# Agent attention and a SoLU feed-forward layer in one kernel: copies of u for float32r transposes, an earlier split of p, a new head, a new place for a product, and a new order

## The chip, the cores and the metric

The kernel runs on one core of one Trainium2 chip. The metric is device time in microseconds (us) of one execution. Before the change the median of three runs is 1497.92 us, the lowest 1496.82 and the highest 1499.42.

## The reference, cut to what matters

There are 4 batches of 12608 tokens with 128 channels, and 49 agents. The 50432 rows that come out of the attention go through a layer of width 1024.

```python
scale = 1 / sqrt(128)
def sm(a, b):                       # softmax of scaled products
    s = scale * (a @ b.T); e = exp(s - s.max(-1)); return e / (e.sum(-1) + 1e-9)
agent_v = sm(agents, k) @ v         # 49 x 128 for each batch
x = sm(q, agents) @ agent_v         # 12608 x 128 for each batch
h = x @ w_in                        # 50432 x 1024
solu = h * softmax(h)
ln = (solu - mean) / sqrt(var + 1e-6) * g_ln
out = ln @ w_out                    # 50432 x 128
```

## The kernel before, in words

**Algebra.** The kernel never forms x. For each batch it forms M = agent_v @ w_in (49 x 1024) and then h = p @ M, where p is the softmax of q against the agents. M is kept as a high and a low part, `mh` and `ml`, in float32r (the form of float32 that TensorE takes in one pass), and p as a high and a low part stacked on the partitions. The mean and the gain of the normalisation are folded into w_out (`w2`, and its parts `wH` and `wL`), so that only the factor of each row (from the sums S and Q of `c_exp` and `c_sq`) is left for the end.

**Phase a** (`phase_a`), once for each batch: 13 chunks of k and v. Products with k into PSUM (L465), maximum on VectorE, exponential on ScalarE (L491), transposes (L498), a copy (L504), products with v (L514). For batch 0 (the head) the loads of k and v go in turn, one chunk of each, into borrowed buffers.

**Phase b** (`phase_b`), once for 8 tiles of 128 tokens: products of q with the agents (L694), softmax on VectorE and ScalarE, the product with the reciprocal on GpSimd into `pack` (L722), two float32 transposes for 4 tiles (L729), a copy on ScalarE (`pf`, L737), the split into high and low on GpSimd (L743, L748), and 4 transfers that put the parts into place in `pT` (L767).

**The main loop** goes over 396 tiles of 128 tokens. For a tile x: `c_h` (L824, four float32r products with 512 columns into one of two PSUM tiles `ph`), `c_max` on VectorE (L828), `c_exp` on ScalarE (L838), `c_u` on VectorE (L843: u = h times e), `c_sq` on ScalarE (L849). Then u must be transposed and multiplied by w_out, and there are two ways. Pairs of tiles alternate between them, four tiles make a unit:

- Z tiles (204): `c_t` transposes u with eight 128x128 float32 transposes on TensorE (L856) into two of four PSUM banks `px`; `c_ev` copies them to SBUF on ScalarE (L907); GpSimd splits them into `uH` (L916) and `uL` (L920); `c_w` multiplies a pair of tiles by `wH` and `wL` in 24 float32r products of 256 columns (L937). The output comes out transposed, so the factor of a token stands along the row: `c_rstd` computes it on GpSimd, transposes it on VectorE (L976), sends it to DRAM (L980) and broadcasts it back to all partitions as `rB` (L984). `c_fin` on VectorE multiplies the PSUM bank by `rB` (L1020), which frees the bank, and `c_out` stores it (L1025).
- Y tiles (192): VectorE transposes u in 32x32 blocks (`c_tb`, L863), 16 transfers move the blocks into place (`c_mv`, L871), `c_wy` multiplies in plain float32 (L877, two passes for each of 32 products in a unit). The factor stands on the partitions here; it gets there by a product on GpSimd (`y0`, L1002), a small product on TensorE (`y1`, L1007) and a copy (`y2`, L1011), and `c_fy` applies it on ScalarE or VectorE (L885, L887).

The last 16 tiles have halves that are split directly from PSUM (`c_ldir`), and the last unit takes its factor through TensorE (`d0`, `d1`, `d2`).

**What sets the order.** All of this is registered as operations of a planner (`Plan`). Each has an engine, a cost, a due time, dependencies, and whether it takes or frees one of the four PSUM banks. The planner simulates the engines, including the queue of SyncE (SP), which issues all transfers, and emits each engine's instructions in the order it finds, and the engines keep that order. The due times are the constants `DH`, `DMX`, `DEX` and so on, each with values for the start and the end; `SWITCH`, `HOLD` and `EPS` say how TensorE changes between kinds of work. The planner's cost for four transposes of u is 0.435.

Of the kernel before, what the change touches and what calls it, by code (L numbers as in the profile page):

```python
# [19 lines left out]
class Op:  # L20


    __slots__ = ("eng", "fn", "cost", "due", "left", "outs", "deps", "take", "free", "bank", "start", "end", "by", "ready", "kind", "shy")


class Plan:
# [8 lines left out]
    SWITCH = ((0.0, 0.0, 0.09), (0.0, 0.0, 0.09), (0.15, 0.12, 0.0))  # L35

    HOLD = 0.12

    def __init__(self, banks):
# [4 lines left out]
        self.kind = 0  # L44

# [14 lines left out]
    def push(self, o):  # L60
        o.ready = {}
        for e in o.eng:
            o.ready[e] = max([0.0] + [d.end + (self.LAT.get(d.by + e, 0.2) if d.by != "S" else 0.0) for d in o.deps])
            self.cand[e].append(o)

    def run(self, idle=None):
        while True:
            best = None
            for e, ops in self.cand.items():
                if not ops:  # L70
                    continue
                free = [b[0] for b in self.banks if b[0] is not None]
                first = min(free) if free else None
                at, opts, low = self.at[e], [], None
                for o in ops:
                    s = max(at, o.ready[e])
                    if o.take:
                        if first is None:
                            continue
                        s = max(s, first)  # L80
                    opts.append((s, o))
                    low = s if low is None else min(low, s)
                if low is None:
                    continue
                near = [z for z in opts if z[0] <= low + self.EPS[e]]
                if e == "P" and self.kind == 2:
                    near = [z for z in opts if z[0] <= low + self.HOLD and z[1].kind == 2] or near
                s, o = min(near, key=lambda z: z[1].due)
                if o.shy > 0.0:
                    s, o = min((z for z in opts if z[0] <= s + o.shy), key=lambda z: z[1].due)  # L90
                if best is None or s < best[0]:
                    best = (s, e, o)
            if best is None:
                break
            s, e, o = best
            for z in o.eng:
                self.cand[z].remove(o)
            if o.take:
# [5 lines left out]
            o.start, o.by = s, e  # L104
            if e == "S":
                hold, size, lag = o.cost
                self.at[e] = s + hold
# [43 lines left out]
def kernel(  # L151
# [25 lines left out]
    CPR = 5.63  # L177
    UTB = 3
# [7 lines left out]
    WC = 4  # L186

    BD0 = 5.03
    BD1 = 15.85
    BD2 = 1.88  # L190
    BD3 = -20.87
    BD4 = -3.24
    BD5 = 3.07
    DH = -9.08
    DMX = 6.59
    DEX = 1.64
    DU_ = -21.8
    DSQ = 15.3
    DT = -0.97
    DEV = 13.79  # L200
    DLD = 12.64
    DSP = 16.84
    DW = 13.2
    DR = 15.79
    DF_ = 37.93
    OUTD = 20.02
    OUTC = -69.6
    VA = 3
    VA1 = 12
    QA = 22.03  # L210
    WA = -7.03
    VLAG = 0.74
    PTB = 4
    SHY = 0.31
    DHR = 5.82
    DHL = -9.02
    DMXR = 19.87
    DMXL = 0.06
    DEXR = -2.43
    DEXL = -3.57  # L220
    DUR = -30.17
    DUL = 17.14
    DSQR = -54.86
    DSQL = 4.96
    DTR = -20.36
    DTL = -14.12
    DEVR = -17.55
    DEVL = 7.51
    DLDR = -20.48
    DLDL = -18.62  # L230
    DSPR = -1.34
    DSPL = -11.65
    DWR = -2.28
    DWL = 3.97
    RBL = 2.38
    ASP = 0.86
    MZ = 5.66
    B7G = True
    B7 = 7.35
    DTB = 4.24  # L240
    DMV = -0.75
    DMS = 0.0
    MVC = 2
    DWY = 11.65
    DWS = 4.05
    YC = 2
    DFY = 5.09
    DTBR = -5.14
    DTBL = -8.26
    ASTART = -4.09  # L250
    AEND = 0.95
# [8 lines left out]
    mpool = ctx.enter_context(tc.tile_pool(name="mpool", bufs=2))  # L260
    bpool = ctx.enter_context(tc.tile_pool(name="bpool", bufs=2))
    epool = ctx.enter_context(tc.tile_pool(name="epool", bufs=3))
    gpool = ctx.enter_context(tc.tile_pool(name="gpool", bufs=ZB))
    ypool = ctx.enter_context(tc.tile_pool(name="ypool", bufs=2))
# [7 lines left out]
    make_identity(nc, ident)  # L272
    ones = const.tile([P, P], F32, name="ones")
# [13 lines left out]
    def pair_f64(dst, names):  # L287
# [5 lines left out]
        def tmp():  # L293
            for k, tg in (("s", "e"), ("a", "e"), ("e", "u"), ("m", "u")):
                t = epool.tile([P, 2, HW], I32, tag=tg, bufs=2, name=f"c{k}_{names}")
                for h in range(2):
                    z[k, h] = t[:, h, :]
# [37 lines left out]
    def load_out():  # L335
        nc.sync.dma_start(out=g_sb, in_=g_ln)
        for h in range(2):
            wd = words["out", h] = mpool.tile([P, HW, 2], I32, tag="mh" if h == 0 else "ml", name=f"wd_out{h}")
# [6 lines left out]
    def conv_out():  # L345
# [8 lines left out]
        def sums(q):  # L354

            n = NF >> (q + 1)
            if q == 0:
                pm["s"] = epool.tile([P, NF // 2, C], F32, tag="sq", bufs=1, name="ws")
# [32 lines left out]
    for i in range(2):  # L391
        pk = const.tile([P, GT, AP2], F32, name=f"pack{i}")
        nc.gpsimd.memset(pk, 0.0)
        packs.append(pk)
# [9 lines left out]
    fold32 = const.tile([P, SQB], F32, name="fold32")  # L404
    nc.vector.tensor_reduce(out=fold32, in_=ident.rearrange("p (a c) -> p c a", c=SQB), op=ALU.add, axis=AX.X)
    quad = const.tile([P, GT], F32, name="quad")
    nc.vector.tensor_reduce(out=quad, in_=ident.rearrange("p (a c) -> p a c", c=SQB), op=ALU.add, axis=AX.X)
    ph2 = [ps_h.tile([P, DF], F32, name=f"ph{i}") for i in range(2)]
    plan = Plan([ps_x.tile([P, HW], F32, name=f"px{i}") for i in range(4)])
    op = plan.op  # L410
# [9 lines left out]
    def phase_a(b, due, gate):  # L420
# [14 lines left out]
        def kload(c):  # L435
            w = CT * P if c < NCK else CKT
            if not head:
                kts[c] = kpool.tile([C, CT * P], F32, tag="kt", name=f"kt{b}_{c}")
            else:
                if c % 4 == 0:  # L440
                    kts["t"] = ypool.tile([C, 4, CT * P], F32, tag="tb", name=f"kh{b}_{c}")
# [3 lines left out]
        def vload(c):  # L445
            if head:
                if c % 4 == 0:
                    vts["t"] = ypool.tile([P, 4, CT, C], F32, tag="uY", name=f"vh{b}_{c}")
# [51 lines left out]
        def p2_et(c, k="D"):  # L500
            px = ps.pop(("t", c))
            w = HW if c < NCK else TX
            eT = res["eT", c] = bpool.tile([P, HW], F32, tag="eT", name=f"eT{b}_{c}")
# [100 lines left out]
        def kop(c):  # L604
            if c < NC and c not in K:
                old = M1.get(c - 1) if not head else M1.get(c - 5 - c % 4)
                K[c] = op("S", st(kload, c), (0.45, sz(c), 0), -199 + 0.2 * c if head else at(c * 2.55 - 3), gate + [old])

        def vop(c):
            old = M2.get(c - 1) if not head else M2.get(c - 5 - c % 4)  # L610
# [4 lines left out]
        FC = {}  # L615
        for c in range(NC):
# [9 lines left out]
            if c:  # L626
                FC[c] = op("A", st(p1_fc, c), 0.2, at(z + 0.6), [N1[c], AC.get(c - 4)])
            TT[c] = op("P", st(p2_t, c), 0.435 * fr(c), at(z + 1), [EE[c], M2.get(c - 2)], take=True)
            ET[c] = (op("A", st(p2_et, c, "A"), 0.478 * fr(c), at(z + 1.2), [TT[c]], free=TT[c]) if head and c < HEADA else
                     op(ETE, st(p2_et, c), (0.478 * fr(c), 0.6 * fr(c)), at(z + 1.2), [TT[c]], free=TT[c]))  # L630
            vop(c)
            M2[c] = op("P", st(p2_mm, c), 0.88 if c < NCK else 0.42, at(z + MZ) if not head else at(z + 1.5),
                       [ET[c], V[c], M2.get(c - 1), AC.get(c - 2)], take=True, kind=2)
            AC[c] = op("D", st(p2_ev, c), 0.26, at(z + 1.8), [M2[c], FC.get(c), AC.get(c - 1)], free=M2[c])
# [17 lines left out]
        for hf in range(2):  # L652
            o8 = op("P", st(f3, hf), 0.86, at(z + 0.5 + 0.4 * hf), [fb] + cin, take=True)
            o9 = op("A", st(f4h, hf), 0.571, at(z + 0.8 + 0.4 * hf), [o8, l0, last_h.get(b - 2)] + mdone[b])
# [26 lines left out]
    def phase_b(k, dues, gate=()):  # L681
# [36 lines left out]

        def b4(q):
            m = min(GT, nt - q * GT)  # L720
            sl = slice(q * GT, q * GT + m)
            nc.gpsimd.tensor_tensor(out=packs[q][:, :m, :A], in0=r["d"][:, sl, :],  # L722
                                    in1=r["s"][:, sl].unsqueeze(2).to_broadcast([P, m, A]), op=ALU.mult)

        def b5(q, px):
            m = min(GT, nt - q * GT)
            r["pt", q] = px
            for j in range(0, m, 2):
                nc.tensor.transpose(px[:, j * AP2 : (j + 2) * AP2], packs[q][:, j : j + 2, :].rearrange("p j a -> p (j a)"),  # L729
                                    ident)  # L730

        def b6(q):
            w = (min(GT, nt - q * GT) + 1) // 2 * P
            r["n", q] = bpool.tile([P, 2, GT // 2 * P], F32R, tag="pn", bufs=2, name=f"pn{b}_{t0}_{q}")
            if B7G:
                r["f", q] = bpool.tile([P, GT // 2 * P], F32, tag="pf", bufs=2, name=f"pf{b}_{t0}_{q}")
                nc.scalar.copy(out=r["f", q][:, :w], in_=r.pop(("pt", q))[:, :w])  # L737
            else:
                nc.scalar.copy(out=r["n", q][:, 0, :w], in_=r["pt", q][:, :w])

        def b7h(q):
            w = (min(GT, nt - q * GT) + 1) // 2 * P
            nc.gpsimd.tensor_scalar(out=r["n", q][:, 0, :w], in0=r["f", q][:, :w], scalar1=1.0, scalar2=0.0, op0=ALU.mult, op1=ALU.add)  # L743

        def b7l(q):
# [498 lines left out]
```

## Time and profile before

| | us |
|---|---|
| median of 3 runs (lowest, highest) | 1497.92 (1496.82, 1499.42) |
| the profiled execution's own time | 1496.0 |
| span of that execution in the trace | 1494.2 |
| TensorE (PE) busy | 1447.1 |
| VectorE (DVE) busy | 1371.5 |
| ScalarE (ACT) busy | 1291.3 |
| GpSimd (POOL) busy | 1110.3 |

The span goes from the first to the last instruction, and the execution's own time has 1.8 us around it. PE's busy time is modelled, since its instructions overlap: for PE one reads how far apart instructions start, and the idle time. PEld are the loads of the stationary operand. Of a wait, the profile gives what ended it. Line numbers (L856) are those of the kernel before.

### The profile page before, as it was taken

The page shows a single profiled execution, that of the slowest core. Times are in us where ns is not written, and L with a number is a line of the kernel's source. Part 1 is how long each engine was busy: PE and PEld are TensorE (multiplying, and loading weights), DVE is VectorE, ACT ScalarE, POOL GpSimd, SP SyncE. Part 2 cuts the span into 40 slices and gives each one's busy share as a digit, 9 for nine tenths or more (in the row PEclk, how much of TensorE's full clock was granted, in tenths as well). Part 3 has the DMA queues.
Part 4 walks back from the last instruction along what each step waited for, and adds up shares of the span by engine and source line. Part 5 has one row for each costly group of instructions (what it writes and reads, how often), then busy time and mean ns, then how long its engine had stood idle before and what let it go on. Part 6 is the DMA issues. An engine that isn't in the chain of part 4 may idle for free.

```text
span 1494.2 us, 34108 instructions
## 1 busy us (share of the span) xinstructions
PE 1447.1 (97%) x11954; PEld 1285.0 (86%) x11954; DVE 1371.5 (92%) x1987; ACT 1291.3 (86%) x2536; POOL 1110.3 (74%) x1569
## 2 busy tenths in 40 slices
PE   8889999999999999999999999899999999999999
PEld 5668889898988989989887888789889898989998
DVE  7799999999999999999998898699999999999996
ACT  4688989889988988899887898688899999999995
POOL 2667787788778777787786677677788888888875
PEclk9999999999999999999999999999999999999999
DMA  9565676676577668756657655567546656566461
GB/s 371 163 179 156 177 186 160 174 184 153 144 194 202 165 179 215 181 137 158 155 140 200 184 156 157 147 175 206 138 118 157 152 126 166 137 154 162 114 155 57
DMA packets 142698, 247.72 MB, mean 166 GB/s; under 512 B 26048, under 2 KB 80320, under 8 KB 142528
## 3 DMA queue, kind: packets, MB, share of 16 engines
q1 hardware_dynamic: 142528, 245.54, 63.1%
q8 instruction: 96, 1.57, 0.5%
q14 instruction: 74, 0.61, 0.1%
HBM read 92.77 MB, written 26.05 MB: 80 GB/s over the span
## 4 chain that ended last, share of the span: by engine, by line
PE 56%; ACT 13%; DVE 10%; DMA 10%; issue 5%; SPq 4%; POOL 2%; DVEq 0%; ACTq 0%; POOLq 0%
PE ph L824 15%; PE px L877 14%; PE px L937 11%; PE px L856 6%; ACT e L838 5%; DVE u L843 4%; DMA rB<-dr 4%; ACT sq L849 4%; DVE nm L828 3%; PE px L465 3%; SPq L871 3%; PE px L514 3%; DMA dr<-yr 2%; ACT uT L907 2%; PE px L694 2%
## 5 line engine op out<-in xcount | busy, mean ns | idle before, releaser
L849 ACT ACTIVATE sq<-u,su 128x1024 bf16<-128x1024 f32 x396 | 460.7, 1163 | 53.4 <-DVE u L843 49.2
L843 DVE SCALAR_TENSOR_TENSOR u<-ph,e 128x1024 f32<-128x1024 f32 x396 | 474.6, 1217 | 29.4 <-ACT e L838 13.6
L838 ACT ACTIVATE e<-ph,nm 128x1024 f32<-128x1024 f32 x396 | 442.8, 1124 | 60.6 <-DVE nm L828 58.9
L828 DVE TENSOR_REDUCE nm<-ph 128x1 f32<-128x1024 f32 x396 | 467.8, 1206 | 28.2 <-PE ph L824 26.8
L920 POOL TENSOR_TENSOR uL<-uT,uH 128x1024 fp32r<-128x1024 f32 (+1 forms) x198 | 470.7, 2377 | 14.5
L877 PE MATMUL px<-w,uY 128*128 128x128 f32 x3072 | 383.0, 276 | 1.7 <-ACT uT L907 1.0
L877 PEld LDWEIGHTS px<-w,uY 128*128 128x128 f32 x3072 | 365.9, 192 | 8.7 <-ACT uT L907 2.3
L824 PE MATMUL ph<-mh,pT 128*128 128x512 f32 x792 | 336.5, 425 | 8.6 <-DVE u L843 5.4
L824 PE MATMUL ph<-ml,pT 128*128 128x512 f32 x792 | 312.8, 395 | 0.0
L916 POOL TENSOR_SCALAR uH<-uT 128x1024 fp32r<-128x1024 f32 (+1 forms) x198 | 207.6, 1048 | 99.2 <-ACT uT L907 99.0
L937 PE MATMUL px<-uH,wH 128*128 128x256 f32 x816 | 238.7, 292 | 0.6 <-POOL x L957 0.3
L863 DVE STREAM_TRANSPOSE tb<-u 128x1024 f32<-128x1024 f32 x192 | 237.2, 1238 | 1.3
L937 PE MATMUL px<-uL,wH 128*128 128x256 f32 x816 | 235.7, 289 | 0.0
L907 ACT COPY uT<-px 128x512 f32<-128x512 f32 x394 | 220.8, 595 | 16.7 <-PE px L856 12.9
L937 PE MATMUL px<-uH,wL 128*128 128x256 f32 x816 | 235.0, 288 | 0.0
L856 PE MATMUL px<-ident,u 128*128 128x128 f32 x1632 | 223.0, 274 | 6.8 <-DVE ob L1020 4.0
L856 PEld LDWEIGHTS px<-ident,u 128*128 128x128 f32 x1632 | 191.2, 141 | 33.4 <-DVE ob L1020 5.1
L824 PEld LDWEIGHTS ph<-mh,pT 128*128 128x128 f32 x792 | 149.8, 189 | 43.7 <-DVE u L843 13.5
L824 PEld LDWEIGHTS ph<-ml,pT 128*128 128x128 f32 x792 | 150.1, 189 | 19.5 <-DVE ml L590 0.3
L937 PEld LDWEIGHTS px<-uH,wL 128*128 128x128 f32 x816 | 153.8, 189 | 5.0 <-issue 2.3
L937 PEld LDWEIGHTS px<-uH,wH 128*128 128x128 f32 x816 | 153.9, 189 | 4.8 <-issue 1.3
L937 PEld LDWEIGHTS px<-uL,wH 128*128 128x128 f32 x816 | 154.1, 189 | 4.2 <-issue 1.1
(132 smaller groups left out, 1595.9 us busy)
## 6 DMA issues: line engine op xcount, KB each, us to landing
uY<-tb SPq DMA_DIRECT2D x768, 128.0 KB, 2.9
pT<-pn SPq DMA_DIRECT2D x392, 64.0 KB, 2.2
qt<-in_qT_dram SPq DMA_DIRECT2D x48, 512.0 KB, 4.4
kt<-in_kT_dram SPq DMA_DIRECT2D x36, 512.0 KB, 4.4
vt<-in_v_dram SPq DMA_DIRECT2D x36, 512.0 KB, 4.8
rB<-dr SPq DMA_DIRECT2D x50, 256.0 KB, 3.7
out_dram<-ob SPq DMA_DIRECT2D x50, 256.0 KB, 2.6
out_dram<-oy SPq DMA_DIRECT2D x48, 256.0 KB, 2.8
```

What stands on the lines that cost most here:

```text
L824: nc.tensor.matmul(ph[:, sl], lhs, bmats[b]["mh" if m == 0 else "ml"][:, sl], start=(m == 0), stop=(m == 1))
L828: nc.vector.tensor_reduce(out=nms[x], in_=phs[x], op=ALU.max, axis=AX.X, negate=True)
L838: nc.scalar.activation(out=es[x], in_=phs[x], func=AF.Exp, bias=nms.pop(x), accum_out=st[G]["S"][:, j : j + 1])
L843: nc.vector.scalar_tensor_tensor(out=u, in0=phs[x], scalar=INV, in1=es[x], op0=ALU.mult, op1=ALU.mult, accum_out=su)
L849: nc.scalar.activation(out=sq, in_=u, func=AF.Square, bias=su, scale=-float(DF), accum_out=st[G]["Q"][:, j : j + 1])
L856: nc.tensor.transpose(pt[:, kf * P : (kf + 1) * P], us[x][0][:, k0 * P : (k0 + 1) * P], ident)
L863: nc.vector.transpose(to, us[x][0].rearrange("p (k r c) -> p k r c", r=GT, c=SQB))
L877: nc.tensor.matmul(st[G]["po"][:, a * P : (a + 1) * P], yb[G][1][:, a, kf].rearrange("p x c -> p (x c)"), w2[:, kf, :], start=(kf == 0), s ...
L907: nc.scalar.copy(out=rr[x][:, hf * 4 : hf * 4 + 4, :], in_=pt)
L916: nc.gpsimd.tensor_scalar(out=uH, in0=rr[x][:, k0:k1, :], scalar1=1.0, scalar2=0.0, op0=ALU.mult, op1=ALU.add)
L920: nc.gpsimd.tensor_tensor(out=uL, in0=rr[x][:, k0:k1, :], in1=uH.bitcast(F32), op=ALU.subtract)
L937: nc.tensor.matmul(po, wt[:, kf, :], ut[:, kf, :], start=(q == 0), stop=(q == WM - 1))
```

## The change

In the order of the diff:

- **Planner.** Five kinds of PE work instead of three in `SWITCH` (two new kinds for `c_w` and `c_wy`); an operation may be marked "SA": issued from SP or from ScalarE's queue, from the latter only right after a long ScalarE operation and 30 us after it was ready. Nearly all due times, `EPS`, `HOLD`, `WC` (12 products of `c_w` at a time instead of 4), `YC` (8 instead of 2) and `MVC` (1 instead of 2) have new values, so the whole order is a new one.
- **u copied for transposes.** A new step `c_cp` copies u of every Z tile (512 KB) with one transfer from SBUF to SBUF into `uR`, a float32r tile (3 buffers); `c_t` transposes `uR` against a float32r identity, as float32r. The planner's cost for four falls from 0.435 to 0.335. u has 3 buffers instead of 2, `uT` 4 instead of 3; the output of `c_sq` goes into the tile of e.
- **p split ahead.** GpSimd multiplies (`b4`) and splits (`b4h`, `b4l`) p before the transposes, 196 elements a partition; `b5` transposes high and low side by side, four float32r transposes for 4 tiles instead of two float32 ones; one ScalarE copy of 512 columns (`b6`) writes `pT`. The 4 transfers for a group of 4 tiles (L767) are gone.
- **Factor of Y units.** `y0`, `y1`, `y2` are replaced by the way of the Z units: a VectorE transpose, a transfer to DRAM, and a transfer (`senty`) back to the partitions.
- **Product by the factor.** `c_fin` remains for the last unit. For the others ScalarE copies the bank to SBUF (`c_fa`), which frees the bank, and GpSimd multiplies by `rB` (`c_fg`). `rB` has 3 buffers, the output tile 1. Both are laid out so that the store is contiguous; the host's unpacking follows.
- **Head.** For batch 0 all loads of k are registered ahead of those of v, and all first passes ahead of the second.

```diff
+    SWITCH = ((0.0, 0.08, 0.17, 0.08, 0.08), (0.0, 0.0, 0.09, 0.02, 0.0), ...
+            if e == "A" and o.eng == "SA":
+                o.ready[e] += self.SLACK
...
         def b4(q):
+            nc.gpsimd.tensor_tensor(out=d, in0=d, in1=rs..., op=ALU.mult)
+        def b4h(q):
+            nc.gpsimd.tensor_scalar(out=packs[q][:, :m, 0, :A], in0=d, ...)
+        def b4l(q):
+            nc.gpsimd.tensor_tensor(out=packs[q][:, :m, 1, :A], in0=d, in1=packs[q][:, :m, 0, :A].bitcast(F32), op=ALU.subtract)
         def b5(q, px):
+            for j in range(m):
+                nc.tensor.transpose(px[:, j * P : (j + 1) * P].bitcast(F32R), packs[q][:, j].rearrange("p i a -> p (i a)"), identR)
         def b6(q):
+            pt = pTs[b, t0 // GT + q] = bpool.tile([P, GT * P], F32R, tag="pT", bufs=PTB, ...)
+            nc.scalar.copy(out=pt[:, : m * P], in_=r.pop(("pt", q))[:, : m * P])
-        def b8(q, i):
...
+    def c_cp(x, e):
+        rr[x, "u"] = rpool.tile([P, DF], F32R, tag="uR", name=f"uR{x}")
+        port[e].dma_start(out=rr[x, "u"].bitcast(F32), in_=us[x][0])
     def c_t(x, hf, pt):
-            nc.tensor.transpose(pt[...], us[x][0][:, k0 * P : (k0 + 1) * P], ident)
+            nc.tensor.transpose(pt[...].bitcast(F32R), rr[x, "u"][:, k0 * P : (k0 + 1) * P], identR)
...
+        def senty(e):
+            yp = st[G]["yp"] = tiny.tile([P, GT], F32, tag="yp", name=f"yp{G}")
+            port[e].dma_start(out=yp, in_=r["dr"].rearrange("j p -> (j p)").rearrange("(a p) -> p a", p=P))
...
+    def c_fa(G):
+        obs[G] = opool.tile([P, GT, GT, SQB], F32, tag="ob", bufs=1, name=f"ob{G}")
+        nc.scalar.copy(out=obs[G].rearrange("d a j c -> d j a c"), in_=st[G]["po", (GT - 1) // 2]...)
+    def c_fg(G):
+        nc.gpsimd.tensor_tensor(out=obs[G], in0=obs[G], in1=st[G]["rB"], op=ALU.mult)
...
-        U[x] = op("D", F(c_u, x), 1.21, ..., [EX[x], T.get((x - 2, 0)), T.get((x - 2, 1)), TBT.get(x - 2), SQ.get(x - 2)])
+        U[x] = op("D", F(c_u, x), 1.21, ..., [EX[x], CP.get(x - UBF), TBT.get(x - UBF), SQ.get(x - UBF)])
+            CP[x] = op("SA", F(c_cp, x), (0.5, 0.524, 0), ..., [U[x], T.get((xo, 0)), T.get((xo, 1))])
-                T[x, hf] = op("P", F(c_t, x, hf), 0.435, ..., [U[x]] + buf, take=True)
+                T[x, hf] = op("P", F(c_t, x, hf), 0.335, ..., [CP[x]] + buf, take=True)
-                FIN[G] = op("D", F(c_fin, G), 0.62, x + DF_, [W[i, 1], RB[G], OZ.get(back(G, 2))], free=pol[G][-1])
+                FA[G] = op("A", F(c_fa, G), 0.5, x + DF_, [W[i, 1], OO.get(back(G, 1))], free=pol[G][-1])
+                FIN[G] = op("G", F(c_fg, G), 0.66, x + DF_, [FA[G], RB[G]])
```

## Rows read from the trace of the kernel before

**Rows 1.** The page: busy time of each engine, and the granted clock

```profile
PE 1447.1 (97%) x11954; PEld 1285.0 (86%) x11954; DVE 1371.5 (92%) x1987; ACT 1291.3 (86%) x2536; POOL 1110.3 (74%) x1569
...
PEclk9999999999999999999999999999999999999999
```

**Rows 2.** Busy us by stage: length, PE, PEld, DVE, ACT, POOL, PEclk, DMA, GB/s

```profile
0.00:100.00 100.00, 85.44 (x755) 56.47 (x756) 80.48 (x154) 61.16 (x134) 47.40 (x71) 0.98 0.71 239
100.00:1450.00 1350.00, 1320.92 (x10892) 1190.75 (x10890) 1261.81 (x1791) 1200.96 (x2349) 1038.49 (x1464) 1.00 0.64 163
...
10.00:40.00 30.00, 30.00 (x283) 17.83 (x280) 26.47 (x54) 14.46 (x38) 9.10 (x8) 1.00 1.03 402
...
1200.00:1300.00 100.00, 98.84 (x811) 89.96 (x811) 95.93 (x129) 93.30 (x182) 83.36 (x117) 1.00 0.63 155
```

**Rows 3.** Timeline of PE, 980 to 996 us: start, length, instruction

```profile
985.14 0.60 PE L856 MATMUL px<-ident,u 128*128 128x128 f32 x4
985.50 0.37 PE L937 MATMUL px<-uH,wL 128*128 128x256 f32 x1
...
986.06 0.28 PE L937 MATMUL px<-uH,wH 128*128 128x256 f32 x1
986.18 0.28 PE L937 MATMUL px<-uL,wH 128*128 128x256 f32 x1
...
986.54 0.40 PE L824 MATMUL ph<-mh,pT 128*128 128x512 f32 x1
986.77 0.39 PE L824 MATMUL ph<-ml,pT 128*128 128x512 f32 x1
...
992.93 1.03 PE L856 MATMUL px<-ident,u 128*128 128x128 f32 x8
993.80 2.40 PE L877 MATMUL px<-w,uY 128*128 128x128 f32 x20
```

**Rows 4.** Tile rB: what its engine waited for, who waited for it

```profile
  DMA rB<-dr: 30.2, 18
...
  PE px L498: 8.6, 2
...
  PE px L856: 4.0, 3
  PE px L729: 2.1, 1
```

**Rows 5.** Groups by form: operations that the change replaces or resembles

```profile
L907 ACT COPY uT<-px 128x512 f32<-128x512 f32 x394 | 220.8, 595 | 16.7 <-PE px L856 12.9 <-POOL z L963 1.7 <-POOL pack L722 0.6
...
L737 ACT COPY pf<-px 128x256 f32<-128x256 f32 x100 | 38.1, 387 | 7.3 <-PE px L729 7.2
...
L1020 DVE TENSOR_TENSOR ob<-px,rB 128x512 f32<-128x512 f32 x50 | 34.2, 684 | 30.2 <-DMA rB<-dr 30.2
...
L976 DVE STREAM_TRANSPOSE yr<-ycol 128x32 f32<-128x32 f32 x50 | 9.9, 197 | 0.0
...
L1011 ACT COPY yp<-px 128x4 f32<-128x4 f32 x34 | 5.6, 165 | 0.7 <-PE px L1007 0.6
...
L308 POOL TENSOR_TENSOR w<-cm_out,ca_out 128x512 f32<-128x512 f32 x2 | 2.5, 1272 | 3.7 <-DVE ca_out L308 3.7
```

**Rows 6.** DMA: one queue's share; issues, KB each, us to landing

```profile
q1 hardware_dynamic: 142528, 245.54, 63.1%
...
uY<-tb SPq DMA_DIRECT2D x768, 128.0 KB, 2.9
pT<-pn SPq DMA_DIRECT2D x392, 64.0 KB, 2.2
...
kt<-in_kT_dram SPq DMA_DIRECT2D x36, 512.0 KB, 4.4
```

**Rows 7.** Groups by form: loads for float32 transposes and float32r products

```profile
L856 PEld LDWEIGHTS px<-ident,u 128*128 128x128 f32 x1632 | 191.2, 141 | 33.4 <-DVE ob L1020 5.1 <-DVE u L843 2.6 <-issue 0.8
L937 PEld LDWEIGHTS px<-uL,wH 128*128 128x128 f32 x816 | 154.1, 189 | 4.2 <-issue 1.1
```

More of the change, by code (lines that the diff above doesn't have):

```diff
@@ L20 @@
 class Op:
-    __slots__ = ("eng", "fn", "cost", "due", "left", "outs", "deps", "take", "free", "bank", "start", "end", "by", "ready", "kind", "shy")
+    __slots__ = ("eng", "fn", "cost", "due", "left", "outs", "deps", "take", "free", "bank", "start", "end", "by", "on", "ready", "kind", "shy")
 class Plan:
@@ L44, in __init__ @@
         self.kind = 0
+        self.long = False
+        self.old = set()
     def op(self, eng, fn, cost, due, deps=(), take=False, free=None, after=(), kind=1, shy=0.0):
@@ L63, in push, with pick @@
             o.ready[e] = max([0.0] + [d.end + (self.LAT.get(d.by + e, 0.2) if d.by != "S" else 0.0) for d in o.deps])
+            if e == "A" and o.eng == "SA":
+                o.ready[e] += self.SLACK
             self.cand[e].append(o)
+            self.old.add(e)
+    def pick(self, e):
+        ops = self.cand[e]
+        if not ops:
+            return None
+        first = None
+        if e == "P":
+            free = [b[0] for b in self.banks if b[0] is not None]
+            first = min(free) if free else None
+        at, opts, low = self.at[e], [], 1e9
+        for o in ops:
+            s = o.ready[e]
+            if o.eng == "SA":
+                if e == "A" and not self.long:
+                    continue
+                if s < at:
+                    s = at
+                if e == "S":
+                    s += self.LEAN
+            elif s < at:
+                s = at
+            if o.take:
+                if first is None:
+                    continue
+                if s < first:
+                    s = first
+            opts.append((s, o))
+            if s < low:
+                low = s
+        if not opts:
+            return None
+        top = low + self.EPS[e]
+        near = [z for z in opts if z[0] <= top]
+        if e == "P" and self.kind:
+            near = [z for z in opts if z[0] <= low + (self.HOLD if self.kind == 2 else self.STICK) and z[1].kind == self.kind] or near
+        s, o = min(near, key=self.rank)
+        if o.shy > 0.0:
+            s, o = min((z for z in opts if z[0] <= s + o.shy), key=self.rank)
+        return s, e, o
@@ L66, in run, with rank @@
+    @staticmethod
+    def rank(z):
+        return z[1].due
     def run(self, idle=None):
+        now, self.old = {}, set(self.cand)
         while True:
+            for e in self.old:
+                now[e] = self.pick(e)
+            self.old = set()
             best = None
[L69 to L92, printed above, removed]
@@ L93, in run @@
+            for e in self.cand:
+                if now[e] is not None and (best is None or now[e][0] < best[0]):
+                    best = now[e]
             if best is None:
@@ L95, in run @@
             s, e, o = best
+            if e == "S" and o.eng == "SA":
+                s -= self.LEAN
+            self.old.add(e)
             for z in o.eng:
                 self.cand[z].remove(o)
+                self.old.add(z)
+            if o.take or o.free is not None:
+                self.old.add("P")
             if o.take:
@@ L445, in vload @@
         def vload(c):
-            if head:
+            if head and c < NCK:
                 if c % 4 == 0:
-                    vts["t"] = ypool.tile([P, 4, CT, C], F32, tag="uY", name=f"vh{b}_{c}")
+                    vts["t"] = ypool.tile([P, 4, CT, C], F32, tag="uY" if c < 4 else "tb", name=f"vh{b}_{c}")
                 vt = vts["t"][:, c % 4]
@@ L732, in b6 @@
         def b6(q):
[L733 to L743, printed above, removed]
```

390 lines of the change are left out of this document (195 added, 195 removed).

## The prediction

> **What bounds the kernel now.** First the page: PE is busy 97% of the span, VectorE 92%, ScalarE 86%, GpSimd 74%, and PE's granted clock is full in every slice, so nothing is to be had from the clock [rows 1]. PE's busy time is modelled, so I go on to the stages. From 100 to 1450 us PE is busy 1321 of 1350 us, VectorE 1262, ScalarE 1201; in one of the fullest stretches, 1200 to 1300, it is 99, 96 and 93 [rows 2]. The head, to 100 us, has 85 us of PE, and from 10 to 40 us the DMA engines are full at 402 GB/s [rows 2]. So in the main loop PE sets the pace, with VectorE close behind and ScalarE next.
>
> Then the timeline of PE, for how far apart its instructions start: eight transposes of u from 992.93 to 993.80, so 0.109 us each; float32r products of 256 columns 0.12 (986.06 to 986.18), of 512 columns 0.23 (986.54 to 986.77); the float32 passes of the Y way about 0.11 (twenty in 2.40) [rows 3]. The rows name float32r operands f32 too. A float32 pass over 128 columns thus takes nearly as long as a float32r pass over 256. Four transposes and the next start take 0.36, but the product behind them is longer, 0.37 instead of 0.28 [rows 3]: 0.45 together, four times 0.109.
>
> Last, the stalls that have one cause: VectorE sat 30.2 us in 18 waits for the transfer of `rB` ahead of `c_fin`, and PE sat 8.6 + 4.0 + 2.1 = 14.7 us behind that for a PSUM bank [rows 4].
>
> I work against the profiled execution, 1496.0 us, 1.9 below the median of the runs; the result is then set on the median.
>
> **The change, part by part.**
>
> Transposes of u, on PE: 204 tiles times 8 = 1632. What a float32r pass over 128 columns takes, the trace doesn't show. From below: half of the 0.12 for 256 columns, about 0.058 by the 0.23 for 512. From above: no gain, 0.109, since something other than the columns may hold the pace. I take the middle, 0.084; the planner's new cost (0.335 for four) is the same figure, and its old one (0.435) is what the trace shows. 1632 x (0.109 - 0.084) = 40.8 us less; between 0 and 83.
>
> Transposes of p, on PE: 200 float32 at 0.109 = 21.8 become one for each of 396 tiles at 0.084 = 33.3: 11.5 more (1 to 21).
>
> `y1` goes: 48 units with two float32 passes of about 0.11: 10.5 less. PE in all: -40.8 + 11.5 - 10.5 = -39.8, from -92 to +11.
>
> `c_fin` leaves VectorE, and the bank is freed by a ScalarE copy that needs no `rB`: the 14.7 us of PE's waits go [rows 4]. What is late next is the product on GpSimd, which now waits for `rB`; behind it there stand the splits of the next tiles. GpSimd is idle a quarter of the span, and `uT` has a fourth buffer; I take 0 for that. The products themselves are 50 x 1.27 = 64 us on GpSimd by the nearest row [rows 5]; the work on `dy` leaves it, and the split of p stays there in another place: covered while GpSimd stays under some 80%.
>
> ScalarE: 50 copies of 512 columns at 0.595 = 30 more; 100 copies for `pT` grow from 0.387 to 0.595, 21 more; `yp` goes, 6 less [rows 5]: +45. VectorE: 34.2 less for `c_fin`, 48 x 0.197 = 9.5 more for the transposes of the factor [rows 5]: -25. In the 1350 us that leaves ScalarE with 1246 and VectorE with 1237, mean 1241.
>
> Transfers: 204 copies of 512 KB add 107 MB; the transfers of `pT` take 26 MB away. At the mean price (63.1% for 245.5 MB [rows 6]) the DMA engines rise from 0.64 to about 0.87 with the shorter span, at the price of the head (402 GB/s) to 0.78. Each copy sits on the path from u to its transposes. The nearest rows are 4.4 us for a load of the same size and 2.9 for 128 KB from SBUF to SBUF [rows 6]. In the loop the third buffer of u hides it: a tile takes 1494/396 = 3.8 us, and u of x is only overwritten at x + 3. Where it is bare is at both ends: little at the start, where VectorE is the slower engine and goes on meanwhile, and most of 4.4 at the end: +5 (0 to 9). SP is in order: behind a copy that waits for u stand the moves of Y tiles, `rB` and stores; but the 392 issues for `pT` [rows 6], which waited there for GpSimd, are gone, so I take 0. Issues by ScalarE happen only 30 us after a transfer was ready, that is hardly ever: 0. The small transfers that replace `y1` (dr and `senty`) land while the unit's 64 float32 passes (7 us) run: 0.
>
> Head: the same bytes through DMA engines that are full: 0, with 3 either way. The new order: 0, since no row shows what it would do.
>
> **Sum.** By PE alone the 1350 us fall by 39.8 + 14.7 = 54.5. But ScalarE and VectorE, which can trade `c_fy` between them, would then be busy 1241 of 1295, 95.8%; the full stretch has 94.6% for their mean [rows 2], and at that share the stretch is 1312, a fall of 38. I take halfway, 46. 1496.0 - 46 + 5 = 1455, and with 1.9 for the median 1457.
>
> The Trainium skill, page "TensorE: Matmul & The Clock Gate", section "Back-to-back issue gap", gives about 81 ns as the sustained spacing of load and product at 128 columns. No run here shows it for float32r; by it the first term would be 46 us instead of 41.
>
> **Rivals.**
>
> *The transposes gain nothing.* A 128-column pass may be held by the load of the stationary operand, which here is u itself, as large as before. For it: the loads of 128 columns for float32r products last 189 ns, those for float32 transposes 141 [rows 7], and no float32r pass with 128 loaded columns starts under 0.12 after the last [rows 3]. Against it: the products that show 0.12 have 256 columns to stream, which explains it as well. Then -0 + 21.4 - 10.5 - 14.7 + 5 = +1: 1499 on the median, at no change.
> The Trainium skill, same page, section "LDWEIGHTS (loading the stationary operand)", gives a load P/1.2 ns for P columns, whatever the rows: 107 ns for 128. By that rule this rival holds; the trace neither shows nor excludes it.
>
> *Slower: the copies come late.* At a DMA share near 0.87 a copy issued behind the 16 transfers of a Y unit lands later than the order assumes, and PE, in order, stands at the transposes. 41 us of gain over 204 tiles are used up at 0.2 us of bare wait for each; with 0.5 the time is 1455 + 102 = 1557, with 0.3, which I take, 1516 (1518 on the median). For it: a far fuller DMA, and an order fixed ahead. Against it: a third buffer, a load of this size in 4.4 us [rows 6], and the 26 MB in small pieces that go.
>
> *ScalarE becomes the bound.* It gets 45 us more and has not been seen above 93.3% [rows 2]: 1246/0.933 = 1335, a fall of 15, so 1486, or 1488 on the median. Against it: the share is low because PE held the loop, and `c_fy` can go to VectorE.
>
> *Better.* The transposes run near 0.058, PE's fall is over 100, and the two others set the time: at 97% busy 1241/0.97 = 1280, a fall of 70: 1431, or 1433.
>
> **Chances and range.** Forecast 0.52, better 0.20, ScalarE's bound 0.12, transposes without gain 0.07, late copies 0.09. A measurement of this kernel can tell about 0.2%, 3 us, from no change. Faster: the first three, 0.84. The case without gain is cut in half between the same and slower, as 1499 stands at the border: with the late copies slower is 0.12, the same 0.04. The range takes in ScalarE's bound above, 1490, and below the two engines at 98% (1241/0.98 = 1267, a fall of 83, 1418): 1420.
>
> **What would show it.** Transposes of `uR` that start about 0.084 apart; PE with no wait on `ob`, and none that the copy of a bank ends late; the 30 us of VectorE's waits for `rB` found on GpSimd; ScalarE's busy time near 1336 and VectorE's near 1347; copies of u landing in 4 to 5 us, and little waiting of PE for them. The prediction is wrong if those transposes stay at 0.11, if PE's longest waits are for `uR`, or if the new order opens gaps on PE that no step above has.

## The result, and the profile after the change

| | before | after |
|---|---|---|
| median (lowest, highest), us | 1497.37 (1493.13, 1499.42) | 1475.78 (1468.71, 1476.69) |
| profiled execution / its span | 1496.0 / 1494.2 | 1468.71 / 1466.2 |

The kernel before has a fourth run here (1493.13), which moves its median from 1497.92 to 1497.37. The ratio is 0.9849, interval 0.9812 to 0.9887: faster by 22 us. The forecast was 1457 in a range from 1420 to 1490. The profiled execution is the fastest of the four, 7 us under their median, at a mean granted clock of 0.996 where the others have 0.991 to 0.994, so times of stages are read from a somewhat good run.

The page of the kernel after: busy times and granted clock, one queue's share, the chain by engine and by line, transfers (KB each, median us to landing).

```profile
PE 1416.2 (97%) x12049; PEld 1242.8 (85%) x12049; DVE 1347.2 (92%) x1973; ACT 1313.8 (90%) x2555; POOL 1134.7 (77%) x1571
...
PEclk9999999999999999999999999999999999999999
...
q1 hardware_dynamic: 142464, 326.73, 75.5%
...
PE 71%; DMA 9%; DVE 7%; ACT 5%; SPq 2%; issue 2%; POOL 1%; DVEq 0%; ACTq 0%; POOLq 0%
PE px L924 21%; PE ph L865 20%; PE px L984 14%; PE px L901 7%; DMA uR<-u 6%; PE px L765 2%; DVE u L884 2%; PE px L575 2%; SPq L918 2%; DVE nm L869 2%; ACT e L879 2%; PE px L521 2%; PE px L810 2%; ACT e L890 1%; ACT uT L954 1%
...
uR<-u SPq DMA_DIRECT2D x204, 512.0 KB, 3.8
uY<-tb SPq DMA_DIRECT2D x768, 128.0 KB, 3.2
...
kt<-in_kT_dram SPq DMA_DIRECT2D x36, 512.0 KB, 5.1
...
rB<-dr SPq DMA_DIRECT2D x50, 256.0 KB, 4.1
```

Against [rows 1], VectorE fell by 24 us, ScalarE rose by 22 and PE fell by 31; the granted clock is at 9 tenths or more in every slice, as before. The queue moves 81 MB more in 75.5% instead of 63.1%, and what shares it lands later: uY in 3.2 us instead of 2.9, the loads of k in 5.1 instead of 4.4 [rows 6]. New in the chain is the copy of u, with 6% of the span.

Busy time by stage of the kernel after: from, to and length, PE, PEld, DVE, ACT, POOL, then granted clock, DMA share and GB/s, as in [rows 2].

```profile
0.00:100.00 100.00, 86.14 (x727) 58.10 (x727) 81.38 (x153) 62.82 (x136) 51.33 (x76) 0.97 0.67 245
100.00:1450.00 1350.00, 1317.49 (x11220) 1172.84 (x11219) 1260.39 (x1812) 1245.87 (x2410) 1078.23 (x1488) 1.00 0.77 225
...
1200.00:1300.00 100.00, 99.97 (x850) 91.12 (x850) 97.97 (x135) 98.40 (x190) 88.84 (x121) 1.00 0.76 218
```

The DMA share of the loop went from 0.64 to 0.77. In the full stretch VectorE and ScalarE are now at 98.0 and 98.4, where they stood at 95.9 and 93.3 [rows 2].

Timeline of PE, kernel after, answering to [rows 3]: start, length, instruction.

```profile
1198.78 0.79 PE L901 MATMUL px<-identR,uR 128*128 128x128 f32 x8
1199.40 2.02 PE L924 MATMUL px<-w,uY 128*128 128x128 f32 x16
...
1201.75 0.81 PE L901 MATMUL px<-identR,uR 128*128 128x128 f32 x8
1202.39 0.46 PE L865 MATMUL ph<-mh,pT 128*128 128x512 f32 x1
1202.69 0.39 PE L865 MATMUL ph<-ml,pT 128*128 128x512 f32 x1
```

Eight float32r transposes and the next start take 0.64 us (1201.75 to 1202.39), 0.08 each. But the product behind them keeps PE for 0.30 instead of its 0.23.

Tile uR of the kernel after: what PE and its loads waited for (us, times), who waited, and the spread of the landing times.

```profile
  DMA uR<-u: 28.1, 23
...
  PE px L901: 19.6, 18
...
  PEld px L901: 8.5, 5
...
DMA to landing us min/median/max: 2.8/3.8/8.7
```

The typical copy is as fast as hoped, but PE and its loads stand 28.1 us in 23 waits for late ones. It is PE's longest wait of one cause, which the prediction named as a sign that it is wrong.

The same view from 100 to 440 us, where most of these waits fall:

```profile
  DMA uR<-u: 18.0, 14
...
DMA to landing us min/median/max: 2.9/4.7/7.5
```

And from 440 to 790 us:

```profile
  DMA uR<-u: 3.8, 2
...
DMA to landing us min/median/max: 2.9/4.6/8.7
```

The copies land no earlier in the second stretch, at the same DMA share (0.78 and 0.79); after 790 us only 2.3 us of waits are left. What differs is the order. From the landing of a copy to the first of its transposes there are 1.7 us in the first stretch and 7.8 in the second (medians, taken from the trace copy by copy). So the copies are late where the order puts their transposes close behind them.

The chain that ended last, kernel after, its five longest pieces: start, length in us, what.

```profile
245.54 6.13 DMA uR<-u
356.97 7.47 DMA uR<-u
424.48 6.19 DMA uR<-u
490.37 7.24 DMA uR<-u
770.44 6.47 DMA uR<-u
```

All five are copies of u, and all lie before 800 us.

Groups by form of the kernel after, as in [rows 5].

```profile
L967 POOL TENSOR_TENSOR uL<-uT,uH 128x1024 fp32r<-128x1024 f32 x196 | 467.9, 2387 | 16.4
...
L901 PEld LDWEIGHTS px<-identR,uR 128*128 128x128 f32 x1632 | 159.4, 140 | 47.7 <-DMA uR<-u 8.5 <-ACT uT L954 7.0 <-issue 5.6
...
L1064 POOL TENSOR_TENSOR ob<-ob,rB 128x512 f32<-128x512 f32 x50 | 64.4, 1288 | 26.6 <-ACT ob L1060 12.9 <-DMA rB<-dr 5.3 <-ACT e L890 4.3
...
L815 ACT CAST pT<-px 128x512 fp32r<-128x512 f32 x96 | 57.7, 601 | 1.9 <-PE px L810 1.3 <-PE ph L865 0.4
...
L1060 ACT COPY ob<-px 128x512 f32<-128x512 f32 x50 | 30.1, 601 | 3.3 <-POOL x L1001 2.1 <-POOL uH L963 0.7 <-issue 0.2
```

The 30.2 us that VectorE waited for `rB` [rows 4] are 5.3 us of GpSimd's.

### The profile page after: what moved, and what is told of

It is laid out like the page before. It is cut to its first block, busy times and chain, and to the rows that moved or that the text cites. A ratio compares the mean times of both kernels' runs of the same rounds, so it can differ in the third digit from the quotient of the medians.

```text
span 1466.2 us, 34026 instructions
## 1 busy us (share of the span) xinstructions
PE 1416.2 (97%) x12049; PEld 1242.8 (85%) x12049; DVE 1347.2 (92%) x1973; ACT 1313.8 (90%) x2555; POOL 1134.7 (77%) x1571
## 3 DMA queue, kind: packets, MB, share of 16 engines
q1 hardware_dynamic: 142464, 326.73, 75.5%
## 4 chain that ended last, share of the span: by engine, by line
PE 71%; DMA 9%; DVE 7%; ACT 5%; SPq 2%; issue 2%; POOL 1%; DVEq 0%; ACTq 0%; POOLq 0%
PE px L924 21%; PE ph L865 20%; PE px L984 14%; PE px L901 7%; DMA uR<-u 6%; PE px L765 2%; DVE u L884 2%; PE px L575 2%; SPq L918 2%; DVE nm L869 2%; ACT e L879 2%; PE px L521 2%; PE px L810 2%; ACT e L890 1%; ACT uT L954 1%
## 5 line engine op out<-in xcount | busy, mean ns | idle before, releaser
L890 ACT ACTIVATE e<-u,su 128x1024 bf16<-128x1024 f32 x396 | 461.8, 1173 | 17.8 <-DVE u L884 17.6
L924 PEld LDWEIGHTS px<-w,uY 128*128 128x128 f32 x3072 | 359.5, 192 | 14.4 <-issue 7.5
L984 PE MATMUL px<-uL,wH 128*128 128x256 f32 x816 | 228.2, 280 | 0.9 <-POOL uL L967 0.9
L984 PE MATMUL px<-uH,wL 128*128 128x256 f32 x816 | 228.2, 280 | 0.0
L954 ACT COPY uT<-px 128x512 f32<-128x512 f32 x394 | 215.6, 600 | 12.3 <-PE px L901 10.6
L901 PEld LDWEIGHTS px<-identR,uR 128*128 128x128 f32 x1632 | 159.4, 140 | 47.7 <-DMA uR<-u 8.5
L901 PE MATMUL px<-identR,uR 128*128 128x128 f32 x1632 | 174.9, 246 | 24.6 <-DMA uR<-u 19.6
```

The lines of the kernel that those rows point to most:

```text
L890: nc.scalar.activation(out=sq, in_=u, func=AF.Square, bias=su, scale=-float(DF), accum_out=st[G]["Q"][:, j : j + 1])
L901: nc.tensor.transpose(pt[:, kf * P : (kf + 1) * P].bitcast(F32R), rr[x, "u"][:, k0 * P : (k0 + 1) * P], identR)
L924: nc.tensor.matmul(st[G]["po"][:, a * P : (a + 1) * P], yb[G][1][:, a, kf].rearrange("p x c -> p (x c)"), w2[:, kf, :], start=(kf == 0), s ...
L954: nc.scalar.copy(out=rr[x][:, hf * 4 : hf * 4 + 4, :], in_=pt)
L984: nc.tensor.matmul(po, wt[:, kf, :], ut[:, kf, :], start=(q == 0), stop=(q == WM - 1))
```

## Experiments: the transposes' pace, and the way of u to them

All keep the order of the changed kernel unless said; line L900 is its L901 where the kernel has a line less. Six runs with the kernel after make a table: the transposes in float32 or float32r, and three sources, the copy, u itself, or a constant, for which they need not wait. The kernels with a constant leave out u: their output is not computed from it.

**Float32 transposes of the copy.**

```diff
-            nc.tensor.transpose(pt[...].bitcast(F32R), rr[x, "u"][...], identR)
+            nc.tensor.transpose(pt[...], rr[x, "u"][...].bitcast(F32), ident)
```

> The changed kernel with one edit: the transposes of uR are done as float32 again (bitcast, float32 identity); copies and the planned order stay. Theory (PE sets the pace; a float32r pass of 128 columns starts 0.083 us after the last against 0.109): 1632 x 0.026 = 42 us come back, less what part of the 28 us of waits for uR is then hidden because PE is later: 1500 to 1516 us, above the kernel before. Rival (ScalarE, VectorE and the DMA engines hold the time, PE's gain is not on the path): under 1488 us.

Measured: 1493.88 us, ratio 0.9961 (0.9945 to 0.9978), between the two expectations: against the 0.9849 after, the faster pace is worth 17 us, less than half of what 1632 x 0.025 promises.

**Float32r transposes of a constant, no copy.**

```diff
-        rr[x, "u"] = rpool.tile([P, DF], F32R, tag="uR", name=f"uR{x}")
-        port[e].dma_start(out=rr[x, "u"].bitcast(F32), in_=us[x][0])
+        pass
-            nc.tensor.transpose(pt[...].bitcast(F32R), rr[x, "u"][...], identR)
+            nc.tensor.transpose(pt[...].bitcast(F32R), identR, identR)
```

> Leaves out the data of u in the Z way: the float32r transposes read a constant, and the copies of u are not issued; the order on every engine stays. Theory (the copies land later than the order assumed, PE stands 20 to 28 us for them): 1448 to 1458 us, with PE's idle time down by 20 us or more. Rival (ScalarE and VectorE are the bound, the waits for uR only take the place of others): 1468 us or more, with PE waiting for ScalarE, VectorE or GpSimd instead.

Measured: 1448.81 us, 0.9671 (0.9653 to 0.9689), as the theory said. Without the copies and without any wait for u the changed kernel would take 27 us less.

**The same, but the copies are issued**, and nobody reads them (only the second line of the last diff).

> As the run without copies, but the copies of u are issued as in the changed kernel and nothing waits for their data: load without wait. Theory (only the wait costs): within 4 us of the run without copies. Rival (the load on the DMA engines and on SP's queue slows the other transfers): nearer to the changed kernel than to the run without copies, with longer waits for rB, yp, k and v.

Measured: 1454.96 us, 0.9721 (0.9696 to 0.9746): 6 us more than without copies (7 by the ratios), above the 4 that were expected. From the page of the run without copies:

```profile
q1 hardware_dynamic: 113088, 219.77, 57.4%
...
uY<-tb SPq DMA_DIRECT2D x768, 128.0 KB, 2.5
...
kt<-in_kT_dram SPq DMA_DIRECT2D x36, 512.0 KB, 4.6
```

From the page of the run with them:

```profile
q1 hardware_dynamic: 142464, 326.73, 76.8%
...
uY<-tb SPq DMA_DIRECT2D x768, 128.0 KB, 3.3
...
kt<-in_kT_dram SPq DMA_DIRECT2D x36, 512.0 KB, 5.3
```

So the 107 MB alone delay other transfers, uY by 0.8 and k by 0.7 us, and cost 6 or 7 us of the 27. The other 20 or so come only when the transposes have to wait for the copies.

**Float32 transposes of u itself**, with 4 buffers of u and no copy (the copy's two lines out, as above, and the pool of `uR` down to 2 buffers).

```diff
-            nc.tensor.transpose(pt[...].bitcast(F32R), rr[x, "u"][...], identR)
+            nc.tensor.transpose(pt[...], us[x][0][...], ident)
```

> The part on u undone with the order kept: float32 transposes read u itself, no copies, four buffers for u. Theory: 42 us of PE more, 20 to 28 us of waits less: 1488 to 1500 us, so the change of the transposes brings 12 to 25 us net, and this kernel stays at or just under the kernel before (the y1 products and the waits for rB are gone there too). Rival (PE's time is not on the path): 1478 us or less.

Measured: 1495.11 us, 0.9976 (0.9964 to 0.9988), as the theory said. But it is no run free of waits: VectorE waits for a free buffer of u. The waits of VectorE in this run (us in total, times, longest):

```profile
DVE u L884 <- PE px L900: 32.4, 16, 3.6
```

**Float32r transposes of u itself**: VectorE writes u as float32r, so no copy is needed (the other edits as in the run before).

```diff
...
+        us[x] = (epool.tile([P, DF], F32R if kind[x] == "Z" else F32, tag="u", bufs=4, ...), ...)
...
+            nc.tensor.transpose(pt[...].bitcast(F32R), us[x][0][...], identR)
```

> The changed kernel, its order of work kept, without the copies of u: in the tiles whose u is transposed VectorE writes u as float32r itself (so the sum over u there sees values rounded to float32r), the transposes read u, and u has 4 buffers, which are held until the transposes are done. Theory (the waits for the copies are what keeps the change from the 1449 us of the run whose transposes read a constant): 1449 to 1465 us. Rival (VectorE's wait for a free buffer of u takes the place of TensorE's wait for the copy): 1470 us or more.

Measured: 1480.01 us, 0.9881 (0.9848 to 0.9915): the rival. The waits of VectorE in this run:

```profile
DVE u L884 <- PE px L901: 26.0, 14, 3.4
```

The wait for the copy is gone, and a wait of the same size for the buffer stands in its place. The copy's use is thus to give u's buffer back early; its price is its own latency. Which of the two is faster is not told: 0.9849 and 0.9881 lie within each other's intervals.

**Float32 transposes of a constant**, the sixth cell.

```diff
-            nc.tensor.transpose(pt[...].bitcast(F32R), identR, identR)
+            nc.tensor.transpose(pt[...], ident, ident)
```

> As the run whose transposes read a constant and that issues no copies (1449 us), but the transposes are float32 against the float32 identity, as before the change; the order is kept. The output of the Z tiles is not computed from u. Theory (with the slow transposes TensorE's own work hides the waits for u, and the faster pace lays them bare): 1449 plus 1632 x (0.109 - 0.083) = 1491, 1486 to 1495 us, hardly under the 1494 and 1495 us of the two runs with float32 transposes of u and of its copy. Rival (waiting for u costs some 27 us at either pace): 1494 - 27 = 1467, 1462 to 1474 us.

Measured: 1467.47 us, 0.9806 (0.9784 to 0.9827): the rival, at its very number. The table, with ratios to before:

| transposes read | float32 | float32r | difference |
|---|---|---|---|
| a constant | 0.9806 | 0.9671 | 0.0135 (20 us) |
| the copy | 0.9961 | 0.9849 | 0.0112 (17 us) |
| u itself, 4 buffers | 0.9976 | 0.9881 | 0.0095 (14 us) |

The two effects add, as far as the runs can tell (each ratio is good to 0.001 to 0.004). The pace is worth 14 to 20 us whatever the source, and u's way to the transposes by the copy costs 23 us (0.0155) at the old pace and 27 (0.0178) at the new one. So nothing shows that the faster pace laid bare waits that were hidden, as I had supposed; with float32 transposes of the copy, too, PE and its loads waited 26.7 us for it.

These prices are against no wait for u at all. The kernel before had such waits in its own way: PE and its loads stood 4.9 us for u, and VectorE for a buffer of u. The waits of VectorE in the kernel before:

```profile
DVE u L843 <- PE px L856: 9.4, 12, 1.5
```

What they cost at the end no run shows.

Why 20 and not 41, with no wait for u? The timeline of PE in the float32 run of a constant:

```profile
1196.35 1.04 PE L900 MATMUL px<-ident 128*128 128x128 f32 x8
1197.14 0.48 PE L865 MATMUL ph<-mh,pT 128*128 128x512 f32 x1
1197.46 0.40 PE L865 MATMUL ph<-ml,pT 128*128 128x512 f32 x1
```

From the first transpose to the second product 1.11 us, 0.88 without the product's own 0.23. In the kernel after the same takes 0.94 (1201.75 to 1202.69), so 0.71: 0.17 less for a group of eight. Compared group by group over the whole traces of the two runs of a constant, whose PE has the same order, the median saving is 0.07 us for four transposes, 0.16 for eight and 0.25 for twelve, 32 us in all. So 9 us of the forecast are lost, most of it to the slow product behind float32r transposes, which I had counted for float32 alone. Some 12 of the 32 do not reach the end. The waits of PE and its loads that have a releaser (without "issue"), summed over the view of waits, rise from 76.1 to 85.1 us between these two runs, most of it behind VectorE and ScalarE. That names 9 of the 12; the rest is not settled, and is too small for these two runs to tell.

## Experiments: the product, the order, ScalarE

**The product's part alone, in the kernel before.** ScalarE copies the bank, GpSimd multiplies; everything else, the constants of the order too, is the kernel before; the planner places the work anew around the part.

```diff
+    def c_fa(G):
...
+        nc.scalar.copy(out=obs[G]..., in_=st[G]["po", (GT - 1) // 2])
+    def c_fg(G):
...
+        nc.gpsimd.tensor_tensor(out=z, in0=z, in1=st[G]["rB"]..., op=ALU.mult)
...
-                FIN[G] = op("D", F(c_fin, G), 0.62, ..., free=pol[G][-1])
+                FA[G] = op("A", F(c_fa, G), 0.5, ..., free=pol[G][-1])
+                FIN[G] = op("G", F(c_fg, G), 1.25, x + DF_, [FA[G], RB[G]])
```

> The kernel before with one part of the change alone: the product by the factor as a ScalarE copy and a GpSimd product (the planner then places the rest around it). Theory (PE stood 14.7 us for banks that c_fin held while rB was late, and VectorE loses 34 us of work): 1480 to 1488 us, with no wait of PE for ob. Rival (the waits were a matter of the order, and any order not searched for this set of operations costs more than it saves): 1495 us or more.

Measured: 1486.99 us, 0.9916 (0.9895 to 0.9937): 13 us, as the theory said. Tile `rB` in this run, who waited for it (us, times):

```profile
  POOL ob L1030: 2.8, 1
```

**The bank's copy held back until rB has landed.**

```diff
...
+        if "rB" in st[G]:
+            nc.scalar.copy(out=tiny.tile([P, 1], F32, tag="wr", name=f"wr{G}"), in_=st[G]["rB"][:, 0, 0, :1])
         nc.scalar.copy(out=obs[G]..., in_=st[G]["po", (GT - 1) // 2]...)
```

> The changed kernel, its order of work kept, but ahead of ScalarE's copy of the product's bank ScalarE reads one column of the factor's tile rB where the order has rB asked for by then (44 of 50 products), so that the bank is freed only once rB has landed, as it was before the change. About 44 short ScalarE instructions are added, some 10 us of its time. Theory (the product's part of the change pays because the bank no longer waits for rB): waits of TensorE and ScalarE behind rB come back, 1485 to 1495 us. Rival (rB lands in time anyway in the new order, and what pays is VectorE's relief): 1474 to 1480 us.

Measured: 1484.86 us, 0.9918 (0.9892 to 0.9945), 10 us more than the kernel after and just below the theory's range. The group of the added instruction (in an execution of 1492.14 us):

```profile
L1061 ACT COPY wr<-rB 128x1 f32<-128x1 f32 x44 | 9.0, 204 | 12.6 <-DMA rB<-dr 12.6
```

Waiting for `rB` does come back (12.6 us in 5 waits), and ahead of the transposes of u PE and its loads wait 6.1 and 8.7 us for the copy of the bank, against 0 and 1.5 in the kernel after. But the 9.0 us of new ScalarE work would by the next run cost some 6 of the 10, so that this run does not tell the wait from the work. A first form, with the wait ahead of all 50 copies, gave no result: for 6 banks the order asks for `rB` only after the copy. So the 13 us of the run before are shown for the bank and VectorE's relief together, not for each.

**ScalarE's copy of the bank twice.**

```diff
         nc.scalar.copy(out=obs[G]..., in_=st[G]["po", (GT - 1) // 2]...)
+        nc.scalar.copy(out=obs[G]..., in_=st[G]["po", (GT - 1) // 2]...)
```

> The changed kernel, order kept; the ScalarE copy of the bank is done twice (50 x 0.60 = 30 us more on ScalarE). If PE sets the pace and ScalarE has room: 1474 to 1484 us. If ScalarE is the bound, as one of the rivals of the prediction has it: 1498 us or more.

Measured: 1499.17 us, 0.999 (0.9964 to 1.0016): the whole gain is gone. 30 us of ScalarE work cost 21 (0.0141), 0.7 us for each. Part of it may be the bank's price and not ScalarE's, since the second copy holds the bank longer: the waits of PE and its loads for the bank's copy rise from 3 to 11 us. The page:

```profile
PE 1432.5 (96%) x12049; PEld 1248.4 (83%) x12049; DVE 1347.4 (90%) x1973; ACT 1341.7 (90%) x2605; POOL 1133.6 (76%) x1571
```

**Less work on ScalarE**: for 50 tiles the sum of squares takes 256 of 1024 columns and leaves out the rest of the variance.

```diff
+        w = DF // 4 if x % 8 == 0 else DF
...
+        nc.scalar.activation(out=sq, in_=u[:, :w], func=AF.Square, ...
```

> The changed kernel, order kept; on 50 of the 396 tiles the sum of squares on ScalarE takes 256 of 1024 columns (it leaves out the rest of the variance there), about 50 x 0.64 = 32 us less on ScalarE. If ScalarE's work as such holds the time, as the run with the doubled copy suggests (30 us more gave 23): 1448 to 1458 us. If ScalarE has no room for more but is not what holds the time (PE's work and the waits for uR are): 1468 to 1476 us.

Measured: 1479.69 us, 0.9866 (0.9833 to 0.9898), no gain on 0.9849 and 4 us above the range of the second expectation, though the page has ScalarE at 1287.1 us, 27 less. A second copy of the bank is dear, and relieving ScalarE in the sum of squares brings nothing: its work as such is not what holds the loop. PE's waits for the copy in this run:

```profile
PE px L902 <- DMA uR<-u: 29.4, 24, 3.8
```

**The constants of the order before, with all the parts of the change.**

```diff
-    EG = 5.42
-    HLD = -19.21
+    EG = 2.6
+    HLD = 0.12
...
-    WC = 12
+    WC = 4
...
```

(and the due times likewise)

> The changed kernel with all its parts, but with the planner's constants of the kernel before (due times, tolerances, sizes of the pieces; the new step of the copy is due with the transposes). Theory (the parts alone don't bring the gain, the order must be found for them): over 1510 us, slower than the kernel before, with the same busy time of every engine as the changed kernel. Rival (the parts bring it whatever the order): under 1485 us.

Measured: 1562.49 us, 1.042 (1.0375 to 1.0465), as the theory said: 63 us slower than before. PE's longest waits in this run:

```profile
PE px L901 <- DMA uR<-u: 36.5, 33, 2.8
PE ph L865 <- DVE u L884: 28.3, 26, 5.0
```

Together the parts pay only in an order that was found for them. The new order, which I had put at 0, is worth some 86 us to them; what it would do for the kernel before was not tried. Part of the 86 us goes with the clock: the mean granted clock, as a share of full speed, is 0.969 to 0.977 in these runs and 0.991 to 0.996 in the kernel after; a difference of 0.016 is, by estimate, at most 25 us of 1562.

**A planner that expects the copies later** (1.2 us more to landing, due times and tolerances searched anew).

```diff
-                    o.end = self.dma + 0.3
+                    o.end = self.dma + (1.5 if size == 0.524 and hold == 0.5 else 0.3)
...
```

> The changed kernel with one line of the planner altered, a copy of u counts as landed 1.2 us later, and the due times and tolerances searched anew for that. Theory (the waits for uR come from landings that the planner takes to be earlier than they are): PE's waits for uR fall from 28 us to under 10, and the time to 1452 to 1464 us. Rival (a later landing only moves the waits to VectorE and ScalarE): 1470 us or more.

Measured: 1487.33 us, 0.991 (0.9886 to 0.9933), slower than the kernel after. The waits for the copies did not go, and GpSimd got new ones. Tile uR in this run, who waited for it (us, times):

```profile
  PE px L901: 27.0, 24
...
  PEld px L901: 10.9, 11
```

The waits of GpSimd in this run (us in total, times, longest):

```profile
POOL ob L1064 <- DMA rB<-dr: 31.1, 15, 5.6
```

PE's and its loads' waits for the copies thus grew from 28.1 to 37.9 us. Whether a constant added to each copy is the wrong model, or the new search ended at a worse order, this run does not tell. No run made a version that beats the kernel after.

## Why the prediction was right, and where it was not

Direction and range were right; the gain, 22 us, is about half of the 40 forecast.

- **Transposes of u, 40.8 us: the mechanism was right, the size not.** Their pace was put at 0.084 and is 0.08. With the product behind them the work that PE saves is 32 us, and 17 of it were measured at the end (14 to 20 over the three sources).
- **The copies, +5: the step that failed.** "In the loop the third buffer of u hides it" and "Where it is bare is at both ends". The buffer did hide the copy from VectorE, which waits 2.0 us for it. But it does nothing for PE, which has to have the copy: the median landing was near the rows used (3.8 us against 4.4), and it is the late ones that PE meets, with 28.1 us of waits, and in the chain with the longest pieces, 6.1 to 7.5 us. The runs with a constant put the whole price at 27 us, 6 or 7 of it from the load on the queues. Against the 5 of the forecast this term is up to 22 us off, less what the kernel before paid for its own waits for u; the forecast missed by 19. The waits come where the order has the transposes close behind the landing, from 100 to 440 us above all; why the order is so tight there stays open, and the planner that expects the copies later did not help.
- **The product, 14.7 us.** Right in size: 13 us when done alone, though not split between the bank, which the term was for, and VectorE's relief. PE has no wait on the product any more (its loads wait 3.1 us for the bank's copy). That VectorE's 30 us would be found on GpSimd was wrong; they shrank to 5.3.
- **ScalarE 1336, VectorE 1347.** VectorE measured 1347.2. ScalarE's pieces came as priced (30.1 for the bank; 57.7 and 2.0 for `pT`, where `pf` had 38.1), but while all its groups added up rose by 52 us, its busy time, in which neighbours that overlap count once, rose by 22, to 1314.
- **DMA share 0.78 to 0.87.** It is 0.77 in the loop, just under the low end, which was the price of the head (by the rows that price gives rather 0.79 to 0.82).
- **The limit of ScalarE and VectorE.** 94.6% was no ceiling: their mean is 98.2% in the full stretch after. The discount of 8 us that I drew from it stands on a wrong reason, though a discount was due: some 12 us of PE's saving are lost with the constant, too.
- **p and `y1`, +11.5 and -10.5**, and the head, were not run apart. If the parts add (the product was measured in the old order), product -13 and pace -17 make -30, and everything else together costs 8 us, the copies' 27 among it. So the rest, with the new order, gains about 19; how much of that is the waits for u that the kernel before had in its own way was not measured.

Of the rivals, "the transposes gain nothing" fell: they start 0.08 apart. The Trainium skill, page "TensorE: Matmul & The Clock Gate", section "LDWEIGHTS (loading the stationary operand)", would by an estimate from its rule for a load have made that 107 ns; the trace, with 0.08 us, shows that loads of 128 columns did not hold these passes. The 81 ns of the Trainium skill, same page, section "Back-to-back issue gap", agree with the 0.08. "The copies come late" was right in kind: 28.1 us over 204 tiles are 0.14 us each, under the 0.2 from which it decides the sign. "ScalarE becomes the bound" fell with the run that lightened it, though a second copy of the bank cost 0.7 us for each us added.

## What to carry to other kernels

Where a faster instruction needs its operand in another place, price the way there by the late transfers, not by the median, and by how close behind their landing the order puts the reader. Ask also what the way releases: here the copy and a held buffer cost nearly the same. To know what a wait is worth, feed the waiting instruction a constant and keep the order; with two such runs one sees whether two effects add. An order fixed ahead belongs to the work it was planned for: under the old constants all the parts together lost 63 us, though the product alone gained 13.

## What the runs showed of the hardware that was not expected

- A product of 512 columns right behind eight transposes holds PE for 0.30 us (float32r) or 0.32 us (float32) instead of 0.23.
- Loads for float32r transposes last 140 ns, those for float32 ones 141 [rows 7], at spacings of 0.08 and 0.109.
- 107 MB of copies that nobody reads cost 6 or 7 us in this kernel, with the DMA share of the main queue at 76.8%.
- 2% more work on ScalarE, as a second copy of a PSUM bank, took 1.4% of the whole, while relieving it by 2% elsewhere gave nothing.
